# DeltaNet and a maxout layer on one core: the opening rearranged around the first solution

## The chip, the cores and the metric

The kernel runs on one core of a Trainium2 chip. Its engines run side by side, each through its own list of instructions in order, and wait for each other by semaphores: TensorE (PE; PEld are its weight loads), VectorE (DVE), ScalarE (ACT), GpSimd (POOL) and SyncE (SP), which only issues DMAs here. GpSimd and ScalarE issue DMAs too. The metric is the device time of one execution in microseconds, as the median of several runs. TensorE has a granted clock, which the profile gives as a share of full speed.

## What is computed

Two blocks follow each other: a delta-rule attention over batch 4, 8 heads, 768 positions and head width 48, and a feed-forward layer that takes the largest of three products.

```python
k_n = k / (np.linalg.norm(k, axis=-1, keepdims=True) + 1e-06)
for t in range(S):
    y[:, :, t] = einsum('bhd,bhde->bhe', q[:, :, t], state)
    v_old = einsum('bhde,bhd->bhe', state, k_n[:, :, t])
    state = state + beta_t * einsum('bhd,bhe->bhde', k_n[:, :, t], v_t - v_old)
x = y.transpose(0, 2, 1, 3).reshape(B * S, H * D)        # 3072 x 384
h = np.maximum(np.maximum(x @ w1, x @ w2), x @ w3)       # 384 -> 768
out = h @ w_out                                          # 768 -> 384
```

## The kernel before

The sequence is cut into 12 chunks of 64 positions. Inside a chunk the recurrence is a triangular system; its inverse is computed in blocks, and the chunks are then linked by the state. Two chunks make a group; the feed-forward layer runs over a group's 512 tokens (`ffn(m)`), six groups in all. The whole order of work is written out by hand: the program text is the order of each engine's list. While `ffn(m)` runs on TensorE, the steps of the recurrence for the next group are put between its products (tables `FIRST`, `LINKS`, `EARLY_LINKS`).

The opening is what lies ahead of the first `ffn(0)` product (`p_h`, L1303); nothing of the layer can run there. Its steps, in order:

- Loads of keys (`load_k`), queries (`load_q`), values (`load_v`), beta, and the first weight pieces (`fetch`). Each load issues several DMAs on the queue it names; `load_q(n)` writes place n modulo 3, so `load_q(3)` overwrites the queries of `load_q(0)`.
- `turn(n, (0,))` transposes the keys of unit n (a chunk and half of the batch) on TensorE (`p_t`), `turn(n, (1,))` the queries. `keys(n)` is `gram` of keys with keys (`p_g`), copied to `at` and, from unit 4 on, sent to DRAM; `gram(n, (1,), None, later=True)` is keys with queries, copied to `pt` when the function that it returns is called.
- `solve(0)`, a generator stepped by `some(solving, n)`: the first step prepares norms and scales (the square root on ScalarE, small operations on VectorE, the diagonal copied by GpSimd, `norm` as five small operations on GpSimd), and 15 further steps are a product and a difference on VectorE each. For the first group it solves only blocks of 16. At its end, before the change, it turned the solution back (`stream transpose`, L634, two halves) and put it into `ut` by 32-row blocks (`placed`, L557), each copy on a named engine; then it returned. For later groups it goes on to write the solution to DRAM.
- Blocks of 16 become blocks of 32 and then 64. `halves_z(0)`: products `p_e` of `at` with `ut`, copied to `z`. `halves_u(0)`: products `p_f` of `t` (the transposed `ut`, made by `halves_t(0)` in three VectorE transposes, L700 and L702) with `z`, negated into `ut` (L755). `turn_t1(0)`, `join_z(0)` (`p_z`) and `join_u(0)` (`p_j`) do the same one size up.
- `new(0)` (`p_u`), `to_y(0)` (`p_y`), and `to_x(0)` (six transposes `p_x`, copied to `xt`); `xt` is what the first `p_h` waits for.
- Then chunk 1: `placed(1, i)`, `halves_t(1)`, and `solve(1)` for the next group, which reads what `blocks(1)` has loaded.

Chunk 0's products go in two halves of four heads, so that a copy of one half runs beside the products of the other: `heads_of` and `negated_of` give each half its tile and the engine that evacuates it. The tiles come from `ps_two`, three buffers in rotation.

Weights arrive as 64-bit numbers and are converted by the generator `weights()`, stepped by `some(conv, n)`: three ScalarE multiplications for a piece, then `joined`: a shift on VectorE (L266) and an addition on GpSimd (L270). `join_last()` calls `joined` for a piece that waits. `busy(n, ident)` issues n products of the identity with itself that nobody reads. `w_bits` has five buffers, `mant` and `up` two.

Of the kernel before, what the change touches and what calls it, by code (L numbers as in the profile page):

```python
# [23 lines left out]
def kernel(  # L24
# [205 lines left out]
    waiting = []  # L230

    def join_last():
        if waiting:
            joined(*waiting.pop())

    def weights():
# [3 lines left out]
        for n, (dst, _, (a, b)) in enumerate(pieces):  # L240
            if n == 3 * FT:
                join_last()
                yield
            bits = staged.popleft().rearrange("p (a b two) -> p a b two", a=a, two=2)
            low, high = bits[:, :, :, 0], bits[:, :, :, 1]
            mant = work.tile([128, 384], U32, name="mant", bufs=2)
            up = work.tile([128, 384], I32, name="up", bufs=2)
# [7 lines left out]
            nc.scalar.mul(mant_v.bitcast(FP32), high.bitcast(FP32), 2.0**-112)  # L255
            nc.scalar.mul(halves[0], low, 2.0**-29)
            nc.scalar.mul(halves[1], high.bitcast(FP32), 2.0**-64)
            join_last()
# [299 lines left out]

    def solve(m):
# [9 lines left out]
        if m in (0, 2):  # L569
            nc.gpsimd.memset(y_bl, 0.0)  # L570
        elif m > 2:
            nc.scalar.copy(y, zero.to_broadcast(y.shape))
# [14 lines left out]
        if m < 3:  # L587
            norm(k_bl, nt, root)
# [10 lines left out]
        nc.vector.tensor_tensor(out=xb, in0=xb, in1=by, op=ALU.mult)  # L599
        yield  # L600
# [26 lines left out]
        if m == 0:  # L627
            bl_0.append(k_bl)
            back, ahead = in_rows(xs[0]), y.rearrange("p c i -> p i c")
            A, V, P = nc.scalar.copy, nc.vector.tensor_copy, nc.gpsimd.tensor_copy  # L630
            for part, copies in (
                (slice(HB, BL), (P, A, P, A)), (slice(0, HB), (V, P, V, A)),
            ):
                nc.vector.transpose(out=back[:, part], in_=ahead[:, part])  # L634
                for i, copy in enumerate(copies):
                    placed(0, i, copy, part)
            yield
            return
# [65 lines left out]
    def heads_of(c, name, w):  # L704


        copies = (nc.scalar.copy,) if c else (nc.scalar.copy, nc.vector.tensor_copy)
        n = H // len(copies)
        for i, copy in enumerate(copies):
            p_v = ps_two(name)[:, :, 0 : n * w]  # L710
# [5 lines left out]
    def negated_of(c, name, w):  # L716
        if c:
# [3 lines left out]
        p = [  # L721
            ps_two(name)[:, :, 0 : NP * w].rearrange("p g (h x) -> p g h x", x=w)
            for _ in range(3)
        ]
        yield range(NP), (p[0], p[0]), (nc.scalar.mul,) * 2
        yield range(NP, H), (p[1], p[2]), (nc.scalar.mul, nc.vector.tensor_scalar_mul)
# [4 lines left out]
    def halves_z(c):  # L731
# [4 lines left out]
        for hs, p_v, copy in heads_of(c, "p_e", BL):  # L736
# [24 lines left out]
    def join_z(c):  # L761
        at = [ats.pop(2 * c + g) for g in range(2)]
        z, second = zs[c % NU], ut[c % NU][:, :, :, BL:C]
        for hs, p_v, _ in heads_of(c, "p_z", BL):
            for i, h in enumerate(hs):
                for bb, g in TILES:
                    r = block(bb, 1)
                    nc.tensor.matmul(  # L768
                        p_v[block(bb ^ g), g, i], at[g][r, h, 0:BL], second[r, g, h]
                    )  # L770
            for bb in range(2):
                nc.scalar.copy(z[block(bb), :, span(hs)], p_v[block(bb)])
# [101 lines left out]
    def to_x(c):  # L874
# [8 lines left out]
        for g in range(2):  # L883
# [9 lines left out]
            if not c:  # L893
                nc.scalar.copy(xt[:, g], of[:, g])  # L894
# [489 lines left out]
    load_beta_0()  # L1384
    load_k(6)
    load_q(0)
    load_k(7)
    load_q(1)
# [19 lines left out]
    turn(5, (0,))  # L1408
    some(solving, 1)
    keys(4)  # L1410
    keys(5)
    turn(6, (0,))
    turn(0, (1,))
    load_q(3, (nc.gpsimd, nc.gpsimd))
    load_v(0)
    for _ in range(2):
        fetch(nc.sync)
    load_beta()
    keys(6)
    gram(0, (1,), None, later=True)()  # L1420
    turn(7, (0,))
    turn(1, (1,))
    keys(7)
    turn(2, (1,))
    gram(1, (1,), None, later=True)()
    some(conv, 1)
    turn(3, (1,))
    scores = [gram(n, (1,), None, later=True) for n in (2, 3)]
    some(solving, HB + 1)
    for copied in scores:  # L1430
        copied()
    halves_t(0)
    halves_z(0)
    first_norms()
    some(conv, 1)
# [4 lines left out]
    for _ in range(2):  # L1440
        fetch(nc.gpsimd)
# [209 lines left out]
```

## Time and profile before

| | |
|---|---|
| Median of 3 runs | 502.51 us (499.77 to 505.0) |
| Profiled execution | 501.92 us, its span 500.0 us |
| Mean granted TensorE clock | 0.976 |
| TensorE busy | 480.2 us (96%), 8100 products |
| VectorE, ScalarE, GpSimd busy | 348.8, 169.6, 196.1 us |
| DMA moved | 53.51 MB, mean 107 GB/s |
| First solution: VectorE from, to | 16.29, 25.24 us |
| First `p_h` product | 44.06 us |

The trace gives the start and the length of every instruction, the idle time before it and what ended that. Instants are microseconds from the span's start. A fp32 product appears as one or more passes ("x4" of a group counts passes). DMA requests of a queue are listed as issues with a length of their own, and the time from issue to landing is listed apart: a median of 4.1 us for the queries that GpSimd requests in the first 60 us, 6.1 for weight pieces that SP requests.

### The profile page before, as it was taken

Reading aid. Unit: us, or ns where it says so; the run is one execution under the profiler, and the core shown is the slowest. Engines: PE = TensorE matmul, PEld = TensorE weight load, DVE = VectorE, ACT = ScalarE, POOL = GpSimd, SP = SyncE. Lnnn points to the kernel's source line nnn. Section 1 sums busy time; section 2 is a strip of 40 time slices with the busy share of each in tenths; the row PEclk is TensorE's granted clock in tenths of the full one; section 3 lists DMA queues with packets and bytes.
Section 4 is the critical chain, followed back from the end, with each engine's and each line's share of the span. In section 5 each row is a group of like instructions: output and inputs, shape, how many; then the busy total and the mean of one; then the engine's idle time right before and its main releaser. Section 6 shows DMA issues by size and latency. Waiting matters only on the chain.

```text
span 500.0 us, 18781 instructions
## 1 busy us (share of the span) xinstructions
PE 480.2 (96%) x8100; PEld 343.4 (69%) x8100; DVE 348.8 (70%) x819; ACT 169.6 (34%) x329; POOL 196.1 (39%) x330
## 2 busy tenths in 40 slices
PE   7869799999999999999999999999999999999997
PEld 6658688878665556565555565565797457988896
DVE  4888898656697352979552998565998864468753
ACT  5686665985330153201243200252211032212310
POOL 6557684764670394780575870601000020000000
PEclk9767899999999999999999999999999999999999
DMA  8948979874351655543775552833223330330001
GB/s 107 168 100 220 211 178 137 199 218 77 81 144 34 140 117 121 138 126 88 155 129 120 146 135 65 176 50 93 65 68 79 61 72 19 86 77 15 1 16 49
DMA packets 110114, 53.51 MB, mean 107 GB/s; under 512 B 93264, under 2 KB 103920, under 8 KB 110032
## 3 DMA queue, kind: packets, MB, share of 16 engines
q1 hardware_dynamic: 98528, 32.01, 31.8%
q0 software_dynamic: 9088, 19.72, 15.8%
q8 instruction: 64, 1.05, 0.9%
q10 hardware_dynamic: 2416, 0.59, 0.7%
q14 instruction: 18, 0.15, 0.1%
HBM read 39.17 MB, written 13.11 MB: 105 GB/s over the span
## 4 chain that ended last, share of the span: by engine, by line
PE 88%; DVE 3%; DMA 2%; ACT 2%; issue 2%; POOL 1%; SPq 1%; DVEq 0%; POOLq 0%; ACTq 0%
PE p_h L1303 34%; PE p_o L1346 13%; PE p_o L1040 10%; PE p_g L443 5%; PE p_c L1241 4%; PE p_u L826 3%; PE p_y L868 3%; PE p_k L798 2%; PE p_m L960 2%; PE p_t L366 2%; PE p_q L798 2%; PE p_s L849 2%; PE p_j L781 2%; PE p_z L768 2%; PE p_e L1241 1%
## 5 line engine op out<-in xcount | busy, mean ns | idle before, releaser
L1303 PE MATMUL p_h<-xt,w_sb 128*128 128x512 f32 (+1 forms) x468 | 177.7, 523 | 0.6 <-ACT xt L894 0.3
L1303 PEld LDWEIGHTS p_h<-xt,w_sb 128*128 128x128 f32 x468 | 85.1, 191 | 62.0 <-issue 53.0
L1317 DVE TENSOR_TENSOR h<-h,p_h 128x512 f32<-128x512 f32 (+1 forms) x42 | 23.9, 569 | 55.9 <-PE p_h L1303 53.4
L617 DVE TENSOR_TENSOR tmp<-x_bl,y_bl 128x31 f32<-128x31 f32 (+20 forms) x139 | 50.3, 362 | 4.0
L621 DVE TENSOR_TENSOR y_bl<-y_bl,tmp 128x31 f32<-128x31 f32 (+20 forms) x139 | 46.5, 334 | 4.8
L1346 PE MATMUL p_o<-wo_sb,h 128*128 128x384 f32 x144 | 49.2, 490 | 0.4 <-POOL wo_sb L270 0.4
L1313 ACT ACTIVATE h<-p_h 128x512 f32<-128x512 f32 (+1 forms) x30 | 16.6, 552 | 76.2 <-PE p_h L1303 76.2
L401 POOL DMA_DIRECT2D turned<-in_q_dram x72 | 39.2, 552 | 5.1 <-POOL turned L396 2.6
L1346 PEld LDWEIGHTS p_o<-wo_sb,h 128*128 128x128 f32 x144 | 26.8, 190 | 18.5 <-POOL wo_sb L270 1.0
L443 PEld LDWEIGHTS p_g<-kqt 48*64 48x64 f32 x1184 | 23.5, 138 | 11.5 <-issue 7.1
L443 PE MATMUL p_g<-kqt 48*64 48x64 f32 (+1 forms) x1184 | 26.7, 238 | 2.9 <-ACT kqt L372 2.9
L270 POOL TENSOR_TENSOR w_sb<-mant,up 128x384 int32<-128x384 int32 x18 | 18.5, 1032 | 23.7 <-DVE mant L266 20.0
L1352 ACT COPY o_sb<-p_o 128x384 f32<-128x384 f32 x12 | 5.7, 478 | 61.7 <-PE p_o L1346 41.7
L396 POOL MEMSET turned<- 128x96 f32 x18 | 3.3, 190 | 59.1 <-DVE kqt L417 59.1
L653 POOL DMA_DIRECT2D ut<-y_d x4 | 2.6, 651 | 60.4 <-DMA y_d<-y_bl 60.4
L148 POOL DMA_DIRECT2D v_t<-in_v_dram x14 | 11.6, 830 | 28.7 <-PE p_u L826 28.7
L856 DVE TENSOR_TENSOR st<-st,p_s 48x768 f32<-48x768 f32 (+1 forms) x18 | 17.1, 951 | 7.7 <-PE p_s L849 7.3
L810 DVE TENSOR_TENSOR v_t<-v_t,p_k 128x768 f32<-128x768 f32 x11 | 10.4, 949 | 15.3 <-PE p_k L798 15.3
L1346 PE MATMUL p_o<-w_sb,xt 128*128 128x384 f32 x60 | 21.0, 486 | 0.0
L427 DVE TENSOR_TENSOR pt<-p_g,mask 128x512 f32<-128x512 f32 x20 | 13.7, 689 | 10.4 <-PE p_g L443 10.3
L460 ACT COPY at<-p_g 128x512 f32<-128x512 f32 x22 | 12.7, 583 | 18.8 <-DVE pt L427 16.5
L401 POOL DMA_DIRECT2D turned<-in_k_dram x32 | 17.5, 553 | 3.0 <-DMA v_t<-in_v_dram 1.9
(252 smaller groups left out, 917.4 us busy)
## 6 DMA issues: line engine op xcount, KB each, us to landing
w_bits<-in_moe_w_dram SPq DMA_DIRECT2D x9, 384.0 KB, 5.3
w_bits<-in_moe_w_dram POOLq DMA_DIRECT2D x9, 384.0 KB, 4.8
turned<-in_q_dram POOLq DMA_DIRECT2D x72, 48.0 KB, 2.6
out_dram<-o_sb SPq DMA_DIRECT2D x34, 96.0 KB, 2.3
y_x<-y SPq DMA_DIRECT2D x32, 96.0 KB, 2.3
qall<-y_x SPq DMA_DIRECT2D x32, 96.0 KB, 2.9
v_t<-in_v_dram POOLq DMA_DIRECT2D x14, 192.0 KB, 4.5
at_d<-at SPq DMA_DIRECT2D x76, 32.0 KB, 2.9
```

The costliest lines, as they stand in the source:

```text
L270: nc.gpsimd.tensor_tensor(out=dst.bitcast(I32), in0=mant_v.bitcast(I32), in1=up_v, op=ALU.add)
L401: (queue, nc.gpsimd)[i].dma_start(out=t[p0 : p0 + 32, bb, at : at + NP * 2 * D].rearrange("p (j x) -> p j x", j=NP), in_=(k, q)[i][2 * bb ...
L443: nc.tensor.matmul(p_g[rows(bb ^ (g * i)), par, c0 : c0 + C * (1 + whole)], kq[:, 0], kq if whole else kq[:, i],)
L617: nc.vector.tensor_tensor(out=t_v, in0=row.to_broadcast(t_v.shape), in1=column.to_broadcast(t_v.shape), op=ALU.mult,)
L621: nc.vector.tensor_tensor(out=rest, in0=rest, in1=t_v, op=ALU.subtract)
L798: nc.tensor.matmul(p_b[rows(bb), par, c0 : c0 + D], kqt[g][dims(par), j, bb ^ g, i], st[dims(par), bb ^ g, g, j],)
L856: nc.vector.tensor_tensor(out=s_v[r], in0=s_v[r], in1=p_s[r, :, 0 : H * D], op=ALU.add)
L1040: nc.tensor.matmul(to[:, g], a[j][:, 128 * g : 128 * (g + 1)], b[j], start=(start and g == of[0] and j == 0), stop=(stop and g == of[-1] a ...
L1241: nc.tensor.matmul(to, w[stays], moves, start=(n == 0), stop=(n == len(terms) - 1))
L1303: nc.tensor.matmul(p_h, w_sb[i][:, t, f * 128 : (f + 1) * 128], xt[:, t, lo : lo + w], start=(t == 0), stop=(t == KT - 1),)
L1317: nc.vector.tensor_tensor(out=h, in0=h, in1=p_h, op=ALU.max)
L1346: nc.tensor.matmul(p_o, stays, moves, start=(n == 0), stop=(n == len(terms) - 1))
```

## The change

- The queries of unit 0 are requested by GpSimd ahead of k6; SP's list moves up by them. `load_q(3)` moves into the first step of `solve(0)`, behind GpSimd's zeroing, and `turn(0, (1,))` goes ahead of that step.
- `norm` of the first solution is issued after the step and not in it. Two tiles `t` are zeroed by GpSimd.
- The scores of chunk 0's and 1's queries (`gram(0..3, (1,))`) are all copied before the solution ends. Weight fetches and conversions are spread out: `weights()` now stops after every multiplication, so `some(conv, 1)` is one of them (later calls become `some(conv, 3)`), and joins can be up to three pieces behind (`held`), in order of age. The third piece uses room in `wo_sb` for `mant` and `up`.
- The end of `solve(0)` moves out of the generator. `t` for `p_f` is no longer transposed from `ut`: the solution is transposed in one piece (`corners`), and 8 copies of 32x128 put it into the zeroed `t`, three on VectorE, three on GpSimd and two on ScalarE. The second half of the solution is placed first, the first half after `halves_z(0)`.
- `some(solving, HB)` makes one step more than the loop has, and the early return is gone, so `solve(0)` also issues the two DMAs of its solution to DRAM that the other groups use.
- Both halves of `z` are copied by ScalarE; the second half of `p_f` is negated by VectorE alone; the second half of `xt` is copied by VectorE. `join_z` of chunks 0 and 1 works on 64x64 tiles (the added rows are zero) with one copy of 128 rows per half.
- `warmed` issues unread products into a tile ahead of its own: 7, 2, 4, 2, 1 and 1 for `p_e`, `p_f`, `p_z`, `p_j`, `p_u` and `p_y` of chunk 0, and `busy(2)` stands twice around `to_x(0)`: 21 in all, where three stood before.

```diff
-    waiting = []
+    waiting, held = deque(), [2]
...
-            join_last()
+            if len(waiting) > held[0]:
+                join_last()
             waiting.append((dst, mant, mant_v, up_v))
...
+    def turned_back(part):
+        nc.vector.transpose(
+            out=in_rows(xs[0])[:, part],
+            in_=solved[0].rearrange("p c i -> p i c")[:, part],
+        )
+
+    def corners():
+
+        by_column = t1[1].rearrange("p g h x -> p (g h x)").rearrange(
+            "p (c x) -> p c x", x=BL
+        )
+        nc.vector.transpose(out=by_column, in_=solved[0][:, 0:HB])
+        return by_column
+
+    def corner(by_column, i, g, copy):
+        bb, half = divmod(i, 2)
+        copy(
+            fine[0][g][block(bb ^ g, half), :, BL * half : BL * half + HB],
+            by_column[block(bb, half), :, H * g : H * (g + 1)].rearrange(
+                "p c h -> p h c"
+            ),
+        )
...
             nc.gpsimd.memset(y_bl, 0.0)
+            if m == 0:
+                load_q(3, (nc.gpsimd, nc.gpsimd))
...
-        if m < 3:
+        if 0 < m < 3:
             norm(k_bl, nt, root)
...
         nc.vector.tensor_tensor(out=xb, in0=xb, in1=by, op=ALU.mult)
+        if m == 0:
+            solved.extend((y, lambda: norm(k_bl, nt, root)))
+            bl_0.append(k_bl)
         yield
...
+    def warmed(p, n):
+        for _ in range(n):
+            nc.tensor.matmul(p[:, 0, 0:128], ident, ident)
+        return p
+
+    AHEAD = dict(p_e=(7, 0), p_f=(2, 0), p_z=(4, 0), p_j=(2, 0), p_u=(1, 0), p_y=(1, 0))
...
+        for i, engines in enumerate(((A, A), (V, V) if name == "p_f" else (A, V))):
...
+                    if c < 2 * FINE:
+
+                        nc.tensor.matmul(
+                            p_v[rows(bb ^ g), g, i],
+                            at[g][rows(bb), h],
+                            second[rows(bb), g, h],
+                        )
+                        continue
...
+            if c < 2 * FINE:
+                copy(z[:, :, span(hs)], p_v)
+                continue
...
-                nc.scalar.copy(xt[:, g], of[:, g])
+                (nc.scalar.copy, nc.vector.tensor_copy)[g](xt[:, g], of[:, g])
```

The written-out order after it, from keys 4 and 5 to the feed-forward part:

```python
turn(4, (0,)); turn(5, (0,)); turn(0, (1,))
some(solving, 1)
fine[0] = [square("t") for _ in range(2)]
zeros(*fine[0]); solved.pop()(); load_beta()
keys(4); fetch(nc.sync); keys(5); load_v(0)
turn(6, (0,)); gram(0, (1,), None, later=True)(); keys(6); fetch(nc.sync)
turn(1, (1,)); gram(1, (1,), None, later=True)(); turn(2, (1,)); turn(7, (0,))
some(conv, 1); copied = gram(2, (1,), None, later=True); keys(7)
fetch(nc.sync); copied(); some(conv, 1); turn(3, (1,)); some(conv, 1)
gram(3, (1,), None, later=True)(); some(conv, 2); some(solving, HB)
turned_back(second); of_first = corners()
...

turned_back(first); halves_z(0); first_norms()
...
scale(0, nrm_0[:, 0]); load_v(1, nc.gpsimd); halves_u(0); some(conv, 1)
turn_t1(0); join_z(0); join_last(); fetch(nc.gpsimd)
masked(pts[0], by_par(pts[0])); blocks(1, nc.gpsimd); join_u(0)
masked(pts[1], by_par(pts[1])); join_last(); fetch(nc.gpsimd)
old_k(0); old_q(0); new(0); placed(1, 0); placed(1, 1, nc.gpsimd.tensor_copy)
some(conv, 1); to_y(0); some(conv, 2); placed(1, 2); busy(2, ident)
to_x(0); join_last(); busy(2, ident); placed(1, 3); held[0] = 0
halves_t(1); solving = solve(1); some(solving, 1); some(conv, 3)
```

## The prediction

> **What bounds the kernel now.** First view: the page's 40 slices of 12.5 us each (digits are tenths).
>
> ```profile
> PE   7869799999999999999999999999999999999997
> PEclk9767899999999999999999999999999999999999
> ```
>
> TensorE is full from the sixth slice on; the open time is in the first four to five, where its granted clock is low too. Second view, the waits of TensorE after 44 us, where the feed-forward part begins (sum, count, longest, in us):
>
> ```profile
> PE p_k L798 <- issue: 2.4, 1, 2.4
> PE p_o L1346 <- POOL wo_sb L270: 0.4, 1, 0.4
> PE p_h L1303 <- POOL w_sb L270: 0.3, 1, 0.3
> ```
>
> All waits there add up to 5.7 us of 456, and 2.4 are one hole (53.0 to 55.4) that no engine's work explains. So what the opening saves moves everything behind it forward. Third, the chain of waits through the opening (start, length, what):
>
> ```profile
> 29.92 0.70 DVE t L702
> 30.66 0.71 DVE t L702
> 31.39 0.43 DVE z L743
> ...
> 33.73 0.28 ACT ut L755
> 34.13 0.69 PE p_z L768 x30
> ...
> 37.30 2.18 PE p_u L826 x64
> 39.48 1.79 PE p_y L868 x56
> 41.26 1.15 PE p_w L1377 x4
> ```
>
> The first solution ends on VectorE at 25.24; the first `p_h` product is at 44.06. Between lie 18.8 us: first copies and f's transposes on VectorE (to 31.4; second half of `z` is queued behind them), then TensorE at half clock. Fourth, TensorE's busy time and clock between the instants where its clock changed (15.9, 22.7, 29.5, 43.2, 56.9, 60.3: all on one grid of 3.41 us). Columns: length, busy and count of PE, PEld, DVE, ACT, POOL; clock; DMA share; GB/s.
>
> ```profile
> 12.51:15.92 3.41, 1.77 (x68) 1.47 (x68) 3.16 (x6) 2.79 (x7) 1.85 (x3) 0.99 1.12 171
> 22.75:26.16 3.41, 2.37 (x72) 1.82 (x72) 3.07 (x11) 3.34 (x7) 0.00 (x0) 1.00 0.79 146
> 26.16:29.57 3.41, 2.24 (x96) 1.91 (x96) 2.81 (x5) 3.34 (x7) 1.89 (x3) 0.99 1.11 265
> 29.57:32.98 3.41, 2.48 (x71) 2.14 (x64) 3.11 (x7) 2.06 (x6) 0.50 (x1) 0.50 0.19 30
> 36.40:39.81 3.41, 3.16 (x116) 2.92 (x118) 2.23 (x5) 2.25 (x7) 1.92 (x3) 0.50 0.63 201
> 39.81:43.22 3.41, 3.41 (x62) 3.32 (x58) 2.99 (x7) 2.33 (x6) 2.31 (x3) 0.51 0.55 191
> 53.46:56.88 3.42, 1.51 (x15) 1.30 (x15) 1.88 (x5) 2.93 (x8) 1.23 (x2) 0.99 1.13 245
> ```
>
> The reader is to see a rule of this run: the clock fell after intervals with 1.77, 2.24 and 1.51 us busy, held after 2.37, and rose only after a wholly busy one (3.16 was not enough). It was at half from 29.5 to 43.2, the whole critical opening, and for 3.4 us after the hole.
>
> **The change, part by part.**
>
> *Up to 25.24: nothing.* VectorE solves back to back from 16.29, and is released by GpSimd's diagonal copy (15.57 to 16.26). GpSimd now issues q3's two loads (0.71 each) between the zeroing that ends at 14.05 and that copy: to 15.5, while the copy waits for `inv_bl` until 15.43: 0 to 0.1 us. Those loads overwrite q0, so they wait for q0's transposes on TensorE, now after those of keys 4 and 5 (to 11.8). q0's requests move from SP, behind k6, to GpSimd at 5.7 to 7.1 (it is idle until 8.18); at 4.1 us to land (median of q on that queue) it is there at 11.2, 2.5 us before it would hold GpSimd. On SP the k7, q1 and first weight requests go out 1.3 us earlier. The key normalization (5 operations, 1.6 us) and two new zeroings (0.5 each, half of the 0.98 for 1056 columns) stand behind the diagonal copy; beta after them ends near 21, as before.
>
> *Scores.* ScalarE's evacuations (0.53 each) and five single multiplications (0.5) instead of a block of three: 13 and 5 from 14.55 end near 25.3 with the waits for TensorE. The last scores run at 23.9 to 24.6 instead of 26.5 to 27.2, and all `pt` copies are done before the solution; before, two of them (28.34 to 29.4) stood ahead of the transposes. `solve(0)` is now stepped once past its loop, so its write to DRAM is also issued: two requests on SP (0.6 each; SP was idle 31 to 45) and 0.5 MB that nobody reads, at some 200 GB/s 2.6 us of traffic near 28 to 31, where the DMA share was 0.2 to 0.9: nothing, unless an instruction fetch queues behind it (the hole's 2.4 us is the bound).
>
> *Solution to `z`.* VectorE: second half turned 25.24 to 26.26 (1.02, half of 2.03), corners' transpose to 27.0 (0.71, the 128x512 row of L700), three corner copies to 27.9 (0.30, L525), first half turned to 28.9. GpSimd: two placed copies to 27.72 (0.67), three corners 32x128 to 28.9 (no such row: between 0.33, half of its 32x256 copy, and 0.65; taken 0.4, nearer to half, as the elements are half). ScalarE: two placed to 27.75, two corners to 28.3. `p_e` starts at 27.9 as before; its halves take 0.53 each at full clock, `z` follows at 29.0 and 29.55 (was 29.7 and 31.8).
>
> *To `p_u`.* `p_f` waits for corners and `z`: 29.4 to 30.5 (was to 33.3). Its negations: ScalarE four (0.285) after one placed copy, 30.2 to 31.4; VectorE four (0.31) 30.6 to 31.85. `turn_t1` (3 x 0.45) to 33.2. `join_z` uses 64x64 tiles and two `z` copies of 0.39 instead of four of 0.37; `z` at 33.1. `p_j` 33.25 to 34.3, negations to 35.1 (was 37.6 on VectorE). `p_u` 34.75 to 35.85 (1.08 for 64 products at full clock by later `p_y` rows, was 2.18).
>
> *To `p_h`.* `u` 35.9 and 36.5; `p_y` to 37.2; `y` 37.1 and 37.9 (VectorE has one placed copy, 0.6, ahead); two unread products; six transposes to 38.7; `xt` by ScalarE to 38.85 and by VectorE, behind another placed copy, to 39.4. First `p_h` 39.45: **4.6 us earlier, if the clock stays full.**
>
> *The clock and the 21 products.* One unread product is two passes: 0.21 us at full clock (0.107 a pass, as the L366 passes), at half 0.47 (12 passes in 2.93 at the start) to 0.58 (1.15 for two in the chain). The seven ahead of `p_e` fill 24.6 to 26.1, and TensorE still idles 1.8 us. On the grid of this run 26.16 to 29.57 then holds 1.7 us of work, under the 2.24 that let the clock fall. At half clock from 29.57, `p_f` (1.05 per half) ends at 31.25 and four products fill to 33.0: a wholly busy interval, so the clock rises at 32.98. `p_z` comes 1.5 us late, `p_j` 1.3, the first `p_h` at 40.75: 3.3 us earlier. Where the grid lies against the solution is chance, so I take the middle, **4.0 us** (2.1 if the clock comes a stage later, 4.9 if GpSimd's copies are at their low end).
>
> *Later.* `join_z(1)` saves ScalarE 0.58, hidden by TensorE. Multiplications per step stay three. The weights' waits (0.3, 0.4) hang on TensorE's own `p_g` and `p_y` and move with them. The late join of piece 2 (VectorE 39.4, GpSimd to 41) is before its use two steps after 40. 18 products net are 72 more instructions: at most instruction fetches shift.
>
> **Rivals.** *Hole gone (B).* The 2.4 us hole in `p_k` falls 127 products behind a smaller one (48.93) and 127 x 2 ahead of the next (65.15): an instruction-fetch boundary, at DMA shares of 1.1 to 1.2. It shifts by 36 passes and its traffic comes in another order. If it shrinks to the 0.2 to 0.3 of its neighbours, 2.1 are won, and the 3.4 us at half clock after it (some 1.7 lost): 3.8 more, 7.8 in all. Against: the same requests stand at the same steps.
>
> *The clock never falls (C).* If only a long hole lets it fall, the opening gives 4.6: 497.9. Speaks against: it fell at 29.5 with no hole over 1.4 us. The Trainium skill, page "TensorE: Matmul & The Clock Gate", section "Why this matters for your kernels", says that gaps under about 3 us between bursts keep the full clock; by it C would be the forecast. The trace disagrees with it at 29.5, so it gets a small chance.
>
> *Unread products in the way (D), slower.* TensorE runs its stream in order. If the clock falls by 27.9 and no interval gets wholly full before `p_y`, the halves take 1.05 instead of 0.53 and the products 0.47 to 0.58 ahead of each: `p_f` to 33.0, `p_z` to 36.9, `p_j` 39.0, `p_u` 41.6, `p_y` 44.05, `p_h` 46.3, 2.2 us later than now: 504.7. It decides from a clock still at half when `p_u` starts. Against: then TensorE has nearly no idle left, and three wholly busy intervals each raised the clock. The same page, Part 3, says matmuls start and end strictly in program order; the trace shows no product overtaking another.
>
> *Given back (E).* If weights' DMA, not TensorE, sets the pace before 130 us, the two GpSimd waits grow by what was won: 502.5. Against: both hang on TensorE's results.
>
> **Numbers.** The profiled execution took 501.92 (span 500.0), 0.6 under the median 502.51. Forecast: 501.9 - 4.0 = 497.9, on the median 498.5. Chances: forecast (A, 496.5 to 500.5) 0.43; B, 502.5 - 7.8 = 494.7, 0.27; C 0.12; D 0.10; E 0.08. Range 493.8 to 503.5: from B less its spread to short of D. One per cent is 5.0 us, about what this kernel's runs (499.8 to 505.0) can tell from nothing. Faster: B, a quarter of A, half of C: 0.44. Slower by over 1% takes D together with a second hole (2.2 + 3.8 = 6.0): half of D, 0.05. Within: 0.51.
>
> **What would show it.** First `p_h` near 40 (39.4 to 42), `z`'s second half near 29.6, no `t` transposes of f before it, `p_f` ending before 32; the clock down for at most two grid intervals after 27. Wrong if the solution ends later than 25.4 (q0 late), if the clock stays at half to 40, or if waits on `w_sb` of over 1 us appear before 130 us. The hole near `p_k`, gone or not, tells A from B.

## The result, and the profile after

| | median | lowest to highest | ratio to before |
|---|---|---|---|
| before (14 runs) | 501.38 us | 498.97 to 505.0 | 1 |
| changed (14 runs, same chip) | 506.25 us | 502.21 to 509.68 | 1.0102, interval 1.0066 to 1.0138 |
| changed, on another chip (12 runs) | 505.42 us | 503.9 to 508.17 | 1.0045, interval 1.0015 to 1.0075 |

The change makes the kernel slower, by 0.5 to 1.0% depending on the chip. The forecast, 498.5 us or 0.8% faster, was wrong: 506.25 lies above its range of 493.8 to 503.5. The profiled execution of the changed kernel took 503.02 us (span 501.3), near the low end of its runs, so its trace shows less of the loss than the median has. The 40 slices of its page:

```profile
PE   7789799989999999999999999999999999999996
PEclk9987799999999999999999999999999999999999
```

The clock row is fuller in the second and third slice than before (9 and 8 against 7 and 6), but not in the fourth and fifth (7 and 7 against 7 and 8). TensorE's timeline through the opening (start, length, engine, line, what, count, and in brackets the idle time ahead with what ended it):

```profile
23.81 1.83 PE L734 MATMUL p_e<-ident 128*128 128x128 f32 x14
...
29.31 1.75 PE L790 MATMUL p_f<-z,t 64*64 64x32 f32 x64
30.99 2.07 PE L734 MATMUL p_z<-ident 128*128 128x128 f32 x8
33.00 1.13 PE L808 MATMUL p_z<-ut,at 64*64 64x32 f32 x64
34.06 0.71 PE L734 MATMUL p_j<-ident 128*128 128x128 f32 x4
34.70 0.70 PE L831 MATMUL p_j<-z,t 32*32 32x32 f32 x59
36.19 0.25 PE L831 MATMUL p_j<-z,t 32*32 32x32 f32 x5 [0.78 <-issue]
36.37 0.80 PE L734 MATMUL p_u<-ident 128*128 128x128 f32 x2
37.10 1.96 PE L876 MATMUL p_u<-v_t,ut 64*64 64x48 f32 x64
38.99 0.79 PE L734 MATMUL p_y<-ident 128*128 128x128 f32 x2
39.71 1.96 PE L918 MATMUL p_y<-u,pt 64*64 64x48 f32 x64
...
44.48 2.83 PE L1353 MATMUL p_h<-xt,w_sb 128*128 128x256 f32 x12 [0.29 <-DVE xt L944]
```

L734 is the unread products, two passes each. The first `p_h` comes at 44.48, before at 44.06: nothing is won. Between 27.5 and 35.4 TensorE has no idle time left, but from 28.7 on the products' passes stand on the chain of waits: 0.64 us ahead of `p_f`, 2.00 ahead of `p_z`, 0.64 ahead of `p_j`, 0.72 each ahead of `p_u` and `p_y`. Ahead of the last five passes of `p_j` is a hole of 0.78 us in which TensorE waits for nothing that an engine does. Further on, `p_k` has a new wait. The waits of TensorE behind 44 us (sum, count, longest):

```profile
PE p_k L848 <- DVE st L906: 3.1, 1, 3.1
PE p_z L815 <- issue: 1.2, 1, 1.2
PE p_h L1353 <- DVE xt L944: 0.3, 1, 0.3
PE p_h L1353 <- POOL w_sb L280: 0.3, 1, 0.3
```

The hole of 2.4 us in `p_k` is gone, and at the same place TensorE waits 3.1 us for the state addition `st` on VectorE. Before, `p_k` with its hole ended at 55.74, now at 56.18. And the clock, on this run's grid (length, busy and count of the five engines, clock, DMA share, GB/s):

```profile
26.16:29.57 3.41, 2.35 (x85) 2.10 (x88) 3.21 (x7) 3.00 (x7) 2.78 (x6) 1.00 0.78 169
29.57:32.99 3.42, 3.42 (x69) 3.13 (x61) 1.65 (x6) 1.95 (x6) 3.28 (x4) 0.50 0.83 241
32.99:36.40 3.41, 2.63 (x134) 2.32 (x133) 1.78 (x4) 1.49 (x4) 2.91 (x4) 1.00 0.62 153
36.40:39.81 3.41, 3.41 (x76) 2.87 (x76) 2.07 (x5) 1.30 (x3) 2.34 (x4) 0.50 0.74 253
...
56.88:60.29 3.41, 3.41 (x69) 2.61 (x68) 3.31 (x9) 1.93 (x4) 1.00 (x1) 0.50 1.13 227
60.29:63.71 3.42, 3.42 (x62) 2.41 (x66) 3.26 (x10) 2.05 (x4) 2.97 (x3) 0.50 0.75 158
```

The clock fell at 29.6 and rose at 33.0, as the prediction had it; it fell again at 36.4, which it hadn't, and rose at 43.2. After the wait at `p_k` it was at half for two intervals instead of one (56.9 to 63.7; before 56.8 to 60.2), although the first of the two was wholly busy. `p_q`, the next chunk's product with the state, starts at 63.88 and before at 61.80. From there to the end both take nearly the same (437.4 and 438.2 us): what this execution loses, it loses in the first 64 us.

Most of that comes behind the first `p_h`. When `p_f` of the next chunk ends, at 51.88, the changed kernel is 0.24 us ahead of the kernel before (52.12). From there to the end of `p_k` it takes 4.30 us instead of 3.62, and from there to `p_q` 7.70 instead of 6.06. First the changed kernel, then the kernel before:

```profile
55.03 1.15 PE L848 MATMUL p_k<-st,kqt 48*64 48x48 f32 x64 [3.15 <-DVE st L906]
...
58.24 1.93 PE L808 MATMUL p_z<-ut,at 64*64 64x32 f32 x64
60.10 2.93 PE L1353 MATMUL p_h<-xt,w_sb 128*128 128x256 f32 x6
```

```profile
55.37 0.37 PE L798 MATMUL p_k<-st,kqt 48*64 48x48 f32 x9 [2.38 <-issue]
...
57.44 1.08 PE L768 MATMUL p_z<-ut,at 32*32 32x32 f32 x64
58.45 2.42 PE L1303 MATMUL p_h<-xt,w_sb 128*128 128x256 f32 x6
```

### The profile page after: what moved, and what is told of

Its sections match the earlier page's. It is cut to its first block, busy times and chain, and to the rows that moved or that the text cites. A ratio compares the mean times of both kernels' runs of the same rounds, so it can differ in the third digit from the quotient of the medians.

```text
span 501.3 us, 18863 instructions
## 1 busy us (share of the span) xinstructions
PE 483.2 (96%) x8136; PEld 346.3 (69%) x8136; DVE 348.8 (70%) x821; ACT 168.5 (34%) x326; POOL 200.0 (40%) x337
## 3 DMA queue, kind: packets, MB, share of 16 engines
q1 hardware_dynamic: 98032, 32.73, 31.7%
## 4 chain that ended last, share of the span: by engine, by line
PE 87%; DVE 6%; DMA 2%; issue 2%; POOL 1%; SPq 1%; ACT 0%; DVEq 0%; POOLq 0%
PE p_h L1353 33%; PE p_o L1396 13%; PE p_o L1090 10%; PE p_c L1291 4%; PE p_g L453 4%; PE p_y L918 3%; PE p_u L876 3%; PE p_k L848 2%; PE p_m L1010 2%; PE p_q L848 2%; PE p_j L831 2%; PE p_t L376 2%; PE p_s L899 1%; PE p_z L815 1%; PE p_e L1291 1%
## 5 line engine op out<-in xcount | busy, mean ns | idle before, releaser
L657 DVE TENSOR_TENSOR tmp<-x_bl,y_bl 128x31 f32<-128x31 f32 (+20 forms) x139 | 49.0, 353 | 4.0
L661 DVE TENSOR_TENSOR y_bl<-y_bl,tmp 128x31 f32<-128x31 f32 (+20 forms) x139 | 48.4, 348 | 4.8
L681 POOL DMA_DIRECT2D ut<-y_d x4 | 2.6, 650 | 60.4 <-DMA y_d<-y_bl 60.3
L148 POOL DMA_DIRECT2D v_t<-in_v_dram x14 | 11.6, 830 | 27.9 <-PE p_u L876 27.9
```

The source lines that it names most:

```text
L657: nc.vector.tensor_tensor(out=t_v, in0=row.to_broadcast(t_v.shape), in1=column.to_broadcast(t_v.shape), op=ALU.mult,)
L661: nc.vector.tensor_tensor(out=rest, in0=rest, in1=t_v, op=ALU.subtract)
```

## The experiments

The theory after the result: the new order of the opening is a gain, and the 21 unread products turn it into a loss (**U**). The rivals: the late VectorE work (**L**), the larger tiles of `join_z` (**W**), the write of the first solution (**Y**). In the expectations Q is U with its reason, the time of the products in order on TensorE. From the fifth on, H is its rival: that the products cost by the instructions which they add. Each kernel was timed in five rounds beside the kernel before, on the same chip; ratios and intervals are to that. The first four kernels, the next four, the next three and the four after them ran on four chips (medians of before: 501.79, 501.48, 503.55, 502.87), and ratios are compared between groups with care: the changed kernel itself has 1.010 on one chip and 1.0045 on another.

**No unread products**

```diff
-    AHEAD = dict(p_e=(7, 0), p_f=(2, 0), p_z=(4, 0), p_j=(2, 0), p_u=(1, 0), p_y=(1, 0))
+    AHEAD = dict(p_e=(0, 0), p_f=(0, 0), p_z=(0, 0), p_j=(0, 0), p_u=(0, 0), p_y=(0, 0))
...
     join_last()
-    busy(2, ident)
+    busy(1, ident)
```

> The changed kernel with no unread products ahead of p_e to p_y and 3 instead of 4 around the transposes, as before the change. Theories: Q, the products cost because TensorE runs them in order at half clock (in the changed kernel's trace p_f to p_y have 4.7 us of them ahead of their own products, 29 to 43 us); L, VectorE's f-transposes for chunk 1 and solve(1)'s preparation were moved behind xt, so the state's addition is late and p_k waits 3.1 us; W, the 64x64 tiles of join_z(1) (1.93 us at half clock against 1.08) keep the clock at half for 3.4 us more; Y, the added write of the first solution to DRAM. Q expects 2 to 4 us less than the changed kernel and the first p_h at 41 to 42.5. L, W and Y expect the same time as the changed kernel within 1 us, or more if the products keep the clock up.

Measured: 500.48 us, ratio 0.9969 (0.9948 to 0.999): faster than the kernel before, and some 0.8 to 1.3% faster than the changed one (by the changed kernel's ratios on its two chips). Its timeline:

```profile
31.53 2.17 PE L808 MATMUL p_z<-ut,at 64*64 64x32 f32 x64 [0.34 <-issue]
33.63 1.47 PE L831 MATMUL p_j<-z,t 32*32 32x32 f32 x64
...
41.74 2.83 PE L1353 MATMUL p_h<-xt,w_sb 128*128 128x256 f32 x12 [0.52 <-DVE xt L944]
...
52.27 1.62 PE L848 MATMUL p_k<-st,kqt 48*64 48x48 f32 x64 [3.13 <-DVE st L906]
```

The clock was at half from 25.4 to 39.1, over the whole critical opening, and the first `p_h` is still 2.3 us earlier than before and 2.7 earlier than in the changed kernel. The reader should set `p_z` beside that of the changed kernel: at half clock it takes 2.17 us, at full clock 1.13. The four products ahead of it, which brought the clock up, took 2.07. They cost twice what they save there. On `p_j`, 59 of the 64 passes took 0.70 where all 64 take 1.47 without the products, and the hole of 0.78 takes that back. The wait for `st` is the same 3.1 us, so it isn't the products' doing. U holds, though Q's reason is tested only further on.

**The old order of VectorE behind `xt`**

```diff
     placed(1, 2)
+    placed(1, 3)
     busy(2, ident)
-    to_x(0)
     join_last()
-    busy(2, ident)
-    placed(1, 3)
     held[0] = 0
     halves_t(1)
     solving = solve(1)
     some(solving, 1)
+    to_x(0)
+    busy(2, ident)
     some(conv, 3)
```

(and both `xt` copies on ScalarE.)

> The changed kernel with the last copy into ut of chunk 1, its f-transposes and solve(1)'s first step put back ahead of the six transposes p_x, and both xt copies back on ScalarE, as before the change. L expects p_k's wait for st (3.1 us) below 0.5, the clock not falling at 56.9, and 3 to 5 us less than the changed kernel; the first p_h at 44 to 46. Q, W and Y expect the same as the changed kernel within 1 us.

Measured: 503.99 us, 1.0056 (1.0027 to 1.0085). The wait for `st` went down only to 1.95 us. In its profiled run the clock was full from 27.1 to 37.3, the very thing that the products are there for, and this is what TensorE did with it:

```profile
33.23 0.78 PE L831 MATMUL p_j<-z,t 32*32 32x32 f32 x59
36.28 0.25 PE L831 MATMUL p_j<-z,t 32*32 32x32 f32 x5 [2.28 <-issue]
...
39.19 1.70 PE L918 MATMUL p_y<-u,pt 64*64 64x48 f32 x54
41.85 0.37 PE L918 MATMUL p_y<-u,pt 64*64 64x48 f32 x10 [0.96 <-issue]
...
44.59 2.83 PE L1353 MATMUL p_h<-xt,w_sb 128*128 128x256 f32 x12 [0.25 <-ACT xt L944]
```

`p_j` began 1.5 us earlier than in the changed kernel and its 60th pass came at the same time: the hole grew from 0.78 to 2.28. It lies at the same pass of the same product, where the program is the same up to there. What TensorE lacks there are its instructions: the trace shows them arriving as packets of 16 KB on a queue of their own, 64 packets for 16,272 matmuls and weight loads, so about 254 instructions or 127 passes in each (counted as 256 and 128 below), and one starts at 33.6 in both runs. The hole ends 2.55 and 2.65 us after that start.

**Smaller tiles in `join_z`**

```diff
-                    if c < 2 * FINE:
+                    if c < 0:
```

(at both places of `join_z`: 32x32 tiles and four copies, as before the change.)

> The changed kernel with join_z of chunks 0 and 1 back on 32x32 tiles and two copies per half. W expects p_z of chunk 1 to take 1.08 at half clock, the clock to rise at 60.3 as before the change instead of 63.7, and 1.5 to 2 us less. Q, L and Y expect the same within 1 us, up to 0.7 more for the additional copies in the opening.

Measured: 505.84 us, 1.0074 (1.0044 to 1.0104), which the changed kernel's two ratios enclose. In its profile the clock was at half for one interval behind `p_k` (59.0 to 62.4), as W had it, but the time isn't less. W isn't what makes it slow; whether the tiles cost or save a few tenths isn't resolved.

**The 21 products in the kernel before**

```diff
+    AHEAD = dict(p_e=(7, 0), p_f=(2, 0), p_z=(4, 0), p_j=(2, 0), p_u=(1, 0), p_y=(1, 0))
...
-            p_v = ps_two(name)[:, :, 0 : n * w]
+            p_v = warmed(ps_two(name), 0 if c else AHEAD[name][i])[:, :, 0 : n * w]
```

(and the same in the branch for the undivided tiles, and `busy(2)` for `busy(1)` behind `to_x(0)`.)

> The kernel before with the 21 unread products of the change at the same places and nothing else. Q expects 2 to 4 us more than before; L, W and Y expect no difference over 1 us; if the products help by holding the clock, 1 to 4 us less.

Measured (7 runs): 507.79 us, 1.0083 (1.0046 to 1.012). First `p_h` at 46.9, `p_k`'s hole of 2.1 still there, and a new hole of 0.67 in `p_y`. The products cost 0.8% in the old order too. U holds from the other side.

**L tried on the kernel without the products**

```diff
     placed(1, 2)
+    placed(1, 3)
+    halves_t(1)
     busy(1, ident)
-    placed(1, 3)
     held[0] = 0
-    halves_t(1)
     solving = solve(1)
```

(and both `xt` copies on ScalarE.)

> The changed kernel without the 18 added unread products (as in the run without them), and with the last copy into ut of chunk 1 and its f-transposes ahead of p_x and both xt copies on ScalarE; solve(1)'s first step stays behind xt. L (late VectorE work delays st, on which p_k waits 3.1 us) expects p_k's wait at 0.5 to 1.5 and 1.5 to 3 us less than without the products alone (500.5), so 497.5 to 499. If the wait costs nothing because the clock or a fetch takes its place: 500 to 501. First p_h up to 0.5 us later than 41.7.

Measured: 499.86 us, 0.997 (0.9946 to 0.9994), not told apart from the kernel without products. The wait for `st` is still 2.5 us: moving f's transposes isn't enough, since `solve(1)`'s preparation stands ahead of `st` too.

**Instructions without work.** Here the kernel without products gets 18 tiny products (32x32x8) ahead of `p_e`, where TensorE idles, so that it has as many TensorE instructions as the changed one.

```diff
-            nc.tensor.matmul(p[:, 0, 0:128], ident, ident)
+            nc.tensor.matmul(p[0:32, 0, 0:8], ident[0:32, 0:32], ident[0:32, 0:8])
...
-    AHEAD = dict(p_e=(0, 0), p_f=(0, 0), p_z=(0, 0), p_j=(0, 0), p_u=(0, 0), p_y=(0, 0))
+    AHEAD = dict(p_e=(18, 0), p_f=(0, 0), p_z=(0, 0), p_j=(0, 0), p_u=(0, 0), p_y=(0, 0))
```

> The changed kernel without the 18 added unread products, and with 18 tiny ones instead (32x32 weights, 8 columns), all in the idle time ahead of p_e: the same number of TensorE instructions as the changed kernel, hardly any array time. Q (array time at half clock in order) expects the time without products, 500.5 within 1 us. H (72 more instructions move the ends of fetched pieces of TensorE's list into p_j and p_y, where holes of 0.8 to 2.3 us without any engine's work were seen) expects a hole near the 59th pass of p_j and 2 to 4 us more, 502.5 to 504.5.

Measured: 504.14 us, 1.0032 (1.0004 to 1.006). Against 0.9969 for the same kernel without the tiny products that is 0.6%, though they end before `p_e` could start:

```profile
24.31 2.08 PE L734 MATMUL p_e<-ident 32*32 32x8 f32 x36
...
37.29 1.79 PE L918 MATMUL p_y<-u,pt 64*64 64x48 f32 x52
39.96 0.66 PE L918 MATMUL p_y<-u,pt 64*64 64x48 f32 x12 [0.88 <-issue]
```

`p_y` starts at 37.29 as without them (37.30); then comes a hole that isn't there without them, the clock stays at half to 43.5 instead of 39.1, and the first `p_h` is at 43.80 instead of 41.74. Of these 2.06 us, 1.34 have come by the end of `p_y`, with the hole, and 0.72 behind it at half clock. So thirty-six passes that take no time on the path cost time by the instructions which they add; that the late clock follows from the hole isn't shown. The kernels on this chip that lack both kinds of products have 0.997 and 0.9977 (the one before this and the next but one).

**Only the seven ahead of `p_e`**

```diff
-    AHEAD = dict(p_e=(0, 0), ...
+    AHEAD = dict(p_e=(7, 0), ...
```

> The changed kernel with only the seven unread products ahead of p_e left (and 3 around the transposes, as before the change): these run while TensorE would idle. Q expects the time without products within 1 us, 500.5, or up to 1 less if they hold the clock; H expects something in between, since 28 of 72 instructions are added: 500.5 to 503.

Measured: 503.05 us, 1.0034 (1.0004 to 1.0063), a hole of 1.33 at `p_u`'s 11th pass, first `p_h` at 43.63. The seven cover idle time only and cost as much as the tiny ones.

**No write of the first solution**

```diff
-    some(solving, HB)
+    some(solving, HB - 1)
```

> The changed kernel without the added unread products and without the two DMAs that write the first solution to DRAM (0.5 MB that nobody reads). Y expects 1 to 2 us less than without the products alone, 498.5 to 499.5, by shorter holes near 35 us; Q, L and H expect 500.5 within 0.7.

Measured on the kernel without products: 499.65 us, 0.9977 (0.9951 to 1.0004): Y not resolved from nothing. The same edit on the changed kernel:

> The changed kernel as it is, without the two DMAs that write the first solution to DRAM. If that write delays the fetch of TensorE's list (in the changed kernel a 16 KB packet of the instruction queue at 33.6 us, usable at 36.2, holds p_j's 59th pass), the hole in p_j shrinks from 0.8 or 2.3 us and the time falls by 1 to 2 us against the changed kernel (506.25). If the holes hang on the number of passes alone, it is the same within 1 us.

Measured: 506.7 us, 1.0062 (1.0034 to 1.0091), within what the changed kernel has. Y isn't resolved as a part of the loss. In the profiled execution of this kernel the clock rose at 32.8 and stayed up to 53.3, which is the course of the forecast:

```profile
34.76 1.03 PE L831 MATMUL p_j<-z,t 32*32 32x32 f32 x64
...
38.01 1.02 PE L918 MATMUL p_y<-u,pt 64*64 64x48 f32 x54
40.15 0.37 PE L918 MATMUL p_y<-u,pt 64*64 64x48 f32 x10 [1.11 <-issue]
...
42.92 2.83 PE L1353 MATMUL p_h<-xt,w_sb 128*128 128x256 f32 x12 [0.30 <-DVE xt L944]
```

`p_j` has no hole (its packet starts at 32.87 and not at 33.64), `p_y` has one, and the first `p_h` comes 1.6 us earlier than in the changed kernel, but still 2.2 after the forecast's 40.75. Then `p_k` waits 3.1 us for `st` as there, the clock is at half from 53.3 to 63.5, and `p_q` starts at 63.80: all that was won is gone again. Whether the missing write made the packet early can't be told from one profile; the second profile of the changed kernel, further down, has the write and no hole in `p_j` either.

**The state addition first.** No products, the early transposes and no write, and `solve(1)` started behind `st`:

```diff
     solving = solve(1)
-    some(solving, 1)
...
-        0: "S1 S1", 1: "e1 s0 S1 S1 S1", 2: "f1 k1 M2 S1 S1",
+        0: "", 1: "e1 s0 S1 S1 S1 S1 S1 S1", 2: "f1 k1 M2 S1 S1",
```

> No added unread products, no write of the first solution, chunk 1's f-transposes and the last copy ahead of p_x, and solve(1) started only behind the state's addition (its six steps of the first two positions all stand behind s0). L expects p_k's wait for st (2.5 us with the transposes early alone) below 0.5, the clock not to fall at 51 to 54 us, and 496 to 498; if a fetch hole takes the wait's place in p_k, 498.5 to 500.

Measured: 503.85 us, 1.002 (0.9988 to 1.0052): not faster. Its timeline at the disputed place:

```profile
49.27 1.01 PE L848 MATMUL p_k<-st,kqt 48*64 48x48 f32 x56
52.55 0.33 PE L848 MATMUL p_k<-st,kqt 48*64 48x48 f32 x8 [2.26 <-issue]
```

The wait for `st` is gone, and a hole of 2.26 us for instructions stands in its place, nearly as large as the one before the change (2.38). At this place two things are late by about the same time, and taking one away shows the other; `p_j` of the next chunk also waits 1.3 us for VectorE, and the clock is at half for four intervals (54.1 to 67.7).

**The same array work in fewer instructions.** Without products, then products up to 512 columns wide: the same columns in 7 products instead of 17 ahead of the chunk's products.

```diff
-        for _ in range(n):
-            nc.tensor.matmul(p[:, 0, 0:128], ident, ident)
+        of = kpad[0].rearrange("p h d -> p (h d)")
+        for w in n:
+            nc.tensor.matmul(p[:, 0, 0:w], ident, of[:, 0:w])
...
+    AHEAD = dict(p_e=((448, 448), ()), p_f=((256,), ()), p_z=((512,), ()), p_j=((256,), ()), p_u=((128,), ()), p_y=((128,), ()))
```

> The array time of the changed kernel's unread products at the same places, but in 7 products of up to 512 columns instead of 17 of 128 (and 3 narrow ones around the transposes): the same number of TensorE instructions as the run with only the seven ahead of p_e (503.05), so the same fetched pieces, with the array time added on the way to p_u. Q expects 2 to 4 us more than that run (505 to 507); H alone expects the same, 503 within 1 us.

Measured: 502.64 us, 0.9989 (0.9953 to 1.0025). The 505 to 507 us that Q expected didn't come. On this chip the changed kernel without its write has 1.0062: the same columns in 11 products fewer are 0.7% faster. Then the same with the products of `p_u` and `p_y` left out and the six `busy` products at the start and two others widened, so that there are as many instructions as in the kernel without products:

> The changed kernel with its unread products as five wide ones (two of 448 columns ahead of p_e, then 256, 512, 256 ahead of p_f, p_z, p_j), and as many instructions taken out: two products of 384 columns instead of six of 128 at the very start, one of 256 instead of two of 128 ahead of p_x, none ahead of p_u and p_y. TensorE's list is as long as without the added products, so its pieces end at the same passes. H (place of the pieces' ends) expects a ratio to before of at most 0.997, 0.992 if the clock is up as well. Q (array time ahead of the real products) expects 1.004 to 1.010.

Measured: 502.8 us, 0.999 (0.9958 to 1.0023). On both chips this is better than the changed kernel (1.0062 without its write, 1.0045; the second pair of intervals just overlaps), and nothing is gained against having no products. Q's 1.004 to 1.010 is missed here too. Executions of the second kernel with a mean clock of 0.990 to 0.992 had spans of 496.6 to 501 us, those at 0.975 to 0.983 had 501 to 504.1; the profiled one is of the second kind, and the longest (half clock from 31.7 to 45.4, `p_h` at 47.14, solution ended 2.9 us late at 27.8). So the executions with more clock are the shorter ones; whether they gain it in the opening wasn't profiled.

**A whole packet more.** If only the place of a packet's end counted, 256 instructions more (64 tiny products in idle times) would put the ends back where they were.

```diff
     turn(7, (0,))
+    tiny(6)
...
     turn(3, (1,))
+    tiny(22)
...
     some(conv, 2)
+    tiny(36)
```

> The changed kernel without the added unread products and with 64 tiny ones, 256 instructions or one whole fetched piece, in TensorE's idle times between 19 and 27 us (6, 22 and 36 of them). H by place expects the ends of the pieces where they are without products and a ratio of 0.996 to 1.000. If the number of instructions counts, more than the 18 tiny ones cost: 1.004 to 1.012.

Measured: 504.27 us, 1.0035 (0.9997 to 1.0073), a hole of 1.27 at `p_u`'s 25th pass, where the kernel without products has none. The theory of the place alone falls: the packet ends at the same pass and `p_u` starts at the same time (35.61 and 35.57), but the packet behind it starts at 34.95 instead of 33.33.

**Everything that had helped**, wide products with even count, early transposes, no write:

> The run with wide products and no net instruction, with chunk 1's f-transposes and last copy ahead of p_x (xt on ScalarE) and without the write of the first solution. Each of these alone was 0 to 0.1 per cent better than without products: H expects 0.990 to 0.996, faster than both kernels; Q expects over 1.002.

Measured: 501.54 us, 0.9972 (0.9941 to 1.0004): short of what H expected, and no better than leaving the products out.

**The changed kernel once more, on this chip**

> The changed kernel itself, on the chip of the three others: every theory expects 1.0066 to 1.0138, as measured first.

Measured: 505.42 us, 1.0045 (1.0015 to 1.0075). This profile (span 503.5) is of another course: no hole ahead of the first `p_h`, and the clock at half from 28.9 to 45.9.

```profile
31.71 2.07 PE L734 MATMUL p_z<-ident 128*128 128x128 f32 x8
33.71 1.93 PE L808 MATMUL p_z<-ut,at 64*64 64x32 f32 x64
35.57 1.22 PE L734 MATMUL p_j<-ident 128*128 128x128 f32 x4
...
46.78 2.83 PE L1353 MATMUL p_h<-xt,w_sb 128*128 128x256 f32 x12 [0.29 <-DVE xt L944]
```

This is what rival D had forecast: a clock still at half when `p_u` starts, and `p_h` at 46.78 where D gave 46.3. It came about otherwise than D had it, though: TensorE was wholly busy in the two intervals from 28.85 to 35.68, and the clock didn't rise. So the same kernel loses in two ways: in this profile the products are 5.7 us of TensorE's time between 28.8 and 41.6, and where the clock came up, holes for instructions stand in the small products. The spans of the two profiles are 1.3 and 3.5 us above that of the kernel before. On the first chip the medians are 4.9 us apart, and an execution that loses as much wasn't profiled.

**How fast instructions arrive**: 320 tiny products behind the last product of the kernel without unread ones; one execution, with its profile.

```diff
+    p_w = ps_ffn([128, TOK], "p_w")
+    for _ in range(320):
+        nc.tensor.matmul(p_w[0:32, 0:8], ident[0:32, 0:32], ident[0:32, 0:8])
     by_hand.close()
```

> The changed kernel without the added unread products, with 320 tiny products (640 passes, five pieces of 128) behind everything else. If TensorE's list arrives in pieces of 128 passes and each is only asked for when the one before is entered, the passes stop every 128 for what the piece still takes: with the other DMAs quiet, pieces every 2 to 4 us; with the 4 to 6 us of the opening, the load of the other DMAs was not what made them slow. If supply is no bound, 640 passes at 0.03 to 0.06 us run through in 19 to 38 us without a hole over 0.3 us.

Measured: 640 passes in 32.23 us without a hole, 0.050 us each, and a packet every 6.8 us. So a packet of 128 passes arrives in 6.4 us or less here, but the passes themselves were too slow to press the supply: the question stays open. Why they were slow is told at the end.

How the runs line up (first `p_h`, `p_q` of the next chunk, span of the profiled run, us):

| | `p_h` | `p_q` | span | span less `p_q` |
|---|---|---|---|---|
| before | 44.06 | 61.80 | 500.0 | 438.2 |
| changed | 44.48 | 63.88 | 501.3 | 437.4 |
| changed, other chip | 46.78 | 65.71 | 503.5 | 437.8 |
| no products | 41.74 | 59.82 | 497.5 | 437.7 |
| no products, 18 tiny | 43.80 | 63.01 | 500.1 | 437.1 |

In these five runs, what is won or lost by `p_q` is the difference of the spans to within 1.1 us. Not all do so: with the old VectorE order the rest took 443.4 us, with larger holes and a further interval at half clock (105.6 to 109.0).

## Why the prediction was wrong

**Up to `p_j`: right.** The solution ended at 24.95 (said 25.24), the halves of `p_e` followed at 26.85 and 27.5 (27.9), `p_f` ended at 31.06 (31.25 with the clock down), the four products at 33.06 (33.0), the clock rose at 33.0 (32.98), and `p_j` started at 34.70 (33.25 plus 1.3: 34.55). The terms of "solution to `z`" and "to `p_u`" were sized well, and one small miss (the three corner copies on VectorE took 1.30 and not 0.9) did no harm. The fall of the clock at 29.6 was partly luck: the prediction counted 1.7 us of work in the interval ahead of it, and there were 2.35, close to the 2.37 at which it had held.

**From `p_j` on: the step that failed is "The clock and the 21 products".** It let the clock rise once and stay up, and priced the products as filling of idle time. Forecast 40.75, measured 44.48: 3.7 us. Stage by stage: 0.15 were late at `p_j`'s start. From there to `p_u` it took 2.40 instead of 1.50 (the hole of 0.78 and `p_u`'s product of 0.72, in place of a wait of 0.45). From `p_u`'s start to `p_y`'s end 4.57 instead of 2.45 (the clock was down again from 36.4, so both took 1.96 instead of 1.08, and `p_y`'s product 0.72). From there to `p_h` 2.81 instead of 2.25 (the products and transposes between at half clock). That is 0.15 + 0.90 + 2.12 + 0.56 = 3.73. The point missed is one of arithmetic: a product in order ahead of work that is ready costs its whole time, and at half clock the four ahead of `p_z` cost 2.00, of which 0.34 would have been idle, to save 1.0. The kernel without products shows it: half clock all the way, and 2.7 us earlier. The clock isn't all of it: in the execution where it did rise once and stay up, the first `p_h` was at 42.92, and 1.55 of the 2.17 us above the forecast lie from `p_u` to the end of `p_y`, where the hole of 1.11 and the product of 0.42 stand.

That the products make the kernel slower is shown from both sides, by taking them out and by adding them to the kernel before. How much of it is their time and how much their number is not settled. Their time is what the two profiles show on the way to `p_h`; but with the same columns in fewer products the loss was gone from the medians (0.9989 and 0.999).

**"18 products net are 72 more instructions: at most instruction fetches shift": the term set at nothing was worth 0.6%.** The tiny products measured it alone: 1.0032, where the two kernels on the same chip without any such products have 0.997 and 0.9977. The hole in `p_k` had been read as a fetch boundary, rightly; what wasn't drawn from it is that a faster clock or an earlier start can turn into a larger hole where 64 passes take 1.1 us. The run with the old VectorE order had the clock up from 27.1 to 37.3, and its first `p_h` at 44.59 instead of the 39.45 that the prediction gives for full clock. That this is a limit of supply fits the twelve holes of 0.7 us and more looked at in ten runs: 2.3 to 3.3 us from a packet's start to the end of its hole, and 3.2 to 6.1 us from the first pass of one packet (128 passes earlier) to the first of the next. But no run isolated it.

**"Later" missed a queue.** It followed `w_sb`, `wo_sb` and the joins and not VectorE behind `xt`: f's transposes for chunk 1 (45.48 to 47.66; before from 42.20) and the preparation of `solve(1)` (47.70 to 51) stand ahead of `st` and now start behind `xt`, and a shift ahead of `st` took 1.77 us (before 1.22). So `st` starts at 54.03 instead of 50.97, and its end at 55.0 is what `p_k` waits for:

```profile
52.34 1.77 DVE L276 TENSOR_SCALAR mant<-mant 128x384 uint32<-128x384 uint32 x1
54.03 0.94 DVE L906 TENSOR_TENSOR st<-st,p_s 128x768 f32<-128x768 f32 x1
```

It took the place of the old hole and is longer, 3.15 us instead of 2.38, and the clock then stayed at half for an interval more. So in this execution 2.3 us are lost between `p_f` and `p_q`, which no term of the prediction held. In the kernel without products the same wait stands, and the clock is at half for one interval (52.7 to 56.2). Taking the wait away gained nothing, since the hole then stood in its place.

**The rivals.** B (hole gone) came about and paid nothing, since a wait of the same size stood behind it: the prediction had asked whether the hole goes, and not what is late next. C (clock never falls) is false: the clock fell at 29.6 after an interval in which the longest idle time was 1.2 us. The rule of the Trainium skill that C drew on, "TensorE: Matmul & The Clock Gate", section "Why this matters for your kernels", that gaps under about 3 us keep the full clock, the trace contradicts here as it did before the change: at 36.4 the clock fell after an interval whose longest gap was the hole of 0.78. D (products in the way) got a chance of 0.10 because three wholly busy intervals had each raised the clock before; its slow course is what happened, in one profile from `p_f` on and in the other from `p_u` on, but beside wholly busy intervals that didn't raise the clock. Its deciding point, a clock still at half when `p_u` starts, was the right one to look at: `p_u` ran at half clock in both. E (given back later) is false: the waits on `w_sb` and `wo_sb` are 0.3 and 0.4 as before.

**The clock rule** (fell at 2.24 us busy or less, held at 2.37, rose after a wholly busy interval) fails in the changed kernel: it fell at 36.4 after 2.63, and at 60.3 it stayed down after 3.41 of 3.41, as it did in the second profile after 28.85 to 35.68. Before, a wholly busy interval from 56.88 did raise it, with `p_z` in 32x32 tiles; there it took 1.08 us of the interval. Since the change it takes 1.93 in 64x64 tiles, and the 128x256 passes of `p_h` have that much less of it.

**Y and W** cost nothing that five rounds can tell.

## What to carry to other kernels

Filling that is to hold the clock up is best kept to times in which the engine would idle: once the next product is ready, each filler stands in its way for its whole time, at half clock twice as long, and that can be set beforehand against what the full clock would save, half the time of the work behind it. Count instructions as well as time: here fillers that lay wholly in idle time cost 0.6%, holes for instructions came up in products of 64 small passes, and the same columns in fewer products cost nothing that the rounds could tell. And where a hole is to go, look at the engine next in line first: here VectorE's addition and the instruction fetch were late by the same two to three microseconds, and each hid the other.

## What the runs showed of the hardware

The larger holes at packet ends of TensorE's instructions were 0.7 to 2.4 us in these runs, up to two ahead of the first `p_h`. The Trainium skill, "Runtime: NRT & Kernel Launch", section "Instruction fetch mechanics", has blocks of 16 KiB and 256 instructions, which agrees with 64 packets of 16 KB for 16,272 matmuls and weight loads, and calls the cost of crossing a block's end mostly hidden, which doesn't: the hole in `p_j` alone is 2.28 us in one run.

The clock doesn't go by the busy share that a profile shows. The tiny products at the end of one kernel kept TensorE shown as busy all the time, and yet (windows of 2 us: length, busy and count of PE, PEld, DVE, ACT, POOL; clock, DMA share, GB/s):

```profile
496.00:498.00 2.00, 2.00 (x51) 1.77 (x50) 0.35 (x1) 0.00 (x0) 0.00 (x0) 1.00 0.53 140
498.00:500.00 2.00, 2.00 (x62) 2.00 (x60) 0.00 (x0) 0.00 (x0) 0.00 (x0) 0.89 0.25 57
500.00:502.00 2.00, 2.00 (x41) 2.00 (x40) 0.00 (x0) 0.00 (x0) 0.00 (x0) 0.50 0.03 8
502.00:504.00 2.00, 2.00 (x41) 2.00 (x40) 0.00 (x0) 0.00 (x0) 0.00 (x0) 0.50 0.00 0
```

it fell at 499.6 and never rose again in 29 us of unbroken passes of 32x32x8, whose own pace went from 62 to 41 in 2 us. That what counts is work in the array and not time shown as busy fits this and the misses of the rule: a busy microsecond of small tiles seems to count less than one of 128x128. How each shape counts wasn't measured.
